# Re-ordering the interleaved attention steps of a fused attention and expert-mixture kernel: query transposes, output buffers, input sums

## Chip, cores and metric

One core of one Trainium2 chip runs the kernel. The metric is the device time of one execution in microseconds (us). TensorE is called PE, VectorE DVE, ScalarE ACT, GpSimd POOL; SyncE (SP) only issues DMAs here, and so does POOL's queue for the loads that cast from float32 to float16.

## What is computed

Attention over 4 batches of 8 heads, 768 positions, 64 wide, in 8 blocks of 96. Keys and values are first mixed across blocks by an 8 x 8 matrix per head, which comes from five rounds of exp and normalization of `sort_net`. Each block of queries then attends to its own mixed block. The output, 3072 tokens by 512, goes through four two-layer networks whose results are mixed by token weights.

```python
k_sorted = einsum('bhij,bhjcd->bhicd', P, k_b)        # P: five rounds on sort_net
v_sorted = einsum('bhij,bhjcd->bhicd', P, v_b)
scores = scale * matmul(q_b, k_sb^T)                  # per block
attn = softmax(scores)
x = matmul(attn, v_sb) -> [B * S, H * D]              # 3072 x 512
p = domain_probs / sum(domain_probs)
for e in range(4):                                    # w1: 512 x 1024, w2: 1024 x 512
    out += p[:, e] * (relu(x @ w1[e]) @ w2[e])
```

## The kernel before

**Two strands in one stream.** The networks are worked in 12 chunks: batch b (0 to 3) times c (0 to 2), 256 tokens each. While the chunks of batches 0 and 1 run, the attention of batches 1, 2 and 3 is woven between their matmuls, so that PE always has something to do. The schedule is written out by hand: instructions stand on each engine in the order of the code, each engine works in that order, and a semaphore wait of one instruction holds all behind it on the same engine.

**A chunk** (`chunk`, `chunk_first`). First the first layer: for each expert two groups of 16 matmuls (L764), each into one of two PSUM buffers of the pool psM, each evacuated by DVE with relu and token weight (L770) into `Hb`. Then the second layer as seven products over half-size blocks in the manner of Strassen (`times`, L749), into four half banks A, B, C and Q of the same two buffers, with sums of `Hb` blocks formed by DVE into `Sb` (`h_sums`, L735 to L741), and additions of the products on DVE (for batch 1: L827, L843, L844, L848, with copies on ACT at L826, L830, L835, L840). At fixed points `slot()` is called, which counts up and runs the attention steps that `PLANS` names for that count: `(c, n, step, batch, pair or half)`. With three experts (batch 0) slots 0 to 5 lie behind the groups of the first layer, with four (batch 1) slots 0 to 7; the later ones lie between the products.

**The attention steps**, per pair of heads (pr, 0 to 3):

- `st_lv`, `st_lk`, `st_n`: loads of values, keys (half a batch each) and queries (two heads each, two DMAs) into regions of the tile `arena`, on POOL's queue (L110, L121). Each region is there once, so the load of the next batch waits for the last reader of this one.
- `st_bv`, `st_bk`: the mixing matrices, built by DVE in `arena` (L335, L327).
- `st_v`: mixed values, two matmuls (L354), which ACT copies into `vo` (L360). After every second pair six DMAs on SP regroup `vo` into `vs`, the "value regroup" (L368).
- `st_q`: transposes a pair's queries from `arena` by a DMA on SP into one of three buffers qT (L375). `st_k`: mixed keys into kT, copied by ACT (L387, L396).
- `st_s`: scores, 16 matmuls (L406), and exp on ACT (L413). `st_a`: 16 matmuls with `vs` (L438), then DVE divides by the sums into `xsl` (L422, L423), one of two buffers. `st_x`: transposes `xsl` by a DMA on SP into the batch's input xT (L454); batch 3's xT lies in `room`.

Scores, outputs, mixed keys and values share a pool of two PSUM buffers, psA. SP's queue carries the regroup, all transposes, the broadcast token weights (`load_p`, L213) and the stores of the outputs (L815), in program order.

**The last six chunks** (batches 2 and 3, `last_chunk`, `seven`) use seven products for the first layer as well (L1025). For these the first-layer weights are summed once: `input_sums(e, n)`, n from 0 to 3 for each of four experts, one DVE instruction each (L961). `s1`, `s3` and `s2` go to blocks of 1024 columns of `arena` (`A_ORDER`), the fourth replaces a quarter of the weights. `PLAN_A` names the slots of batch 1's chunks in which they run, `late_sums` the places inside `last_chunk`. The input sums of expert 2 lie in columns 3072 to 6143 of `arena`, which hold the values of a batch before. `token_sums` (L980) runs in slot 12 of the last ordinary chunk, (1,2), and `last_begin` in slot 13.

```python
    def st_q(b, pr):
        qT = att.tile([P, R, P], F16, name=f"qT_{b}_{pr}", tag="qT", bufs=3)
        nc.sync.dma_start_transpose(
            qT[:], natural[(b, "q")][:, pr].rearrange("p t h d -> p (t h d)")
        )
        qTs[(b, pr)] = qT.rearrange("p t x -> p (t x)").rearrange("p (i x) -> p i x", i=NB)
```

Of the kernel before, what the change touches and what calls it, by code (L numbers as in the profile page):

```python
# [10 lines left out]
F16 = mybir.dt.float16  # L11
# [6 lines left out]
def kernel(  # L18
# [13 lines left out]
    B, H, S, D = q.shape  # L32
    GH = B * H
    NB = sort_net.shape[-1]
    BLK = S // NB
# [3 lines left out]
    P = 128  # L39
# [21 lines left out]
    att = ctx.enter_context(tc.tile_pool(name="att", bufs=2))  # L61
# [5 lines left out]
    def psa(shape, dtype, name):  # L67
        state["n"] += 1
        return psA.tile(shape, dtype, tag="ps", name=name)
# [31 lines left out]
    arena = const.tile([P, 4 * NW + NQ + 4 * 4 * P + R * 4 * VW], F16, name="arena")  # L101
# [317 lines left out]
    def normalize(ps, xsl, hh):  # L419
        av = ps[0:BLK, :, 0:HB * VW].rearrange("c a (i w) -> c a i w", w=VW)  # L420
        rz = att.tile([BLK, 2, HB, 1], F32, name=f"rz_{state['n']}", tag="rz", bufs=4)
        nc.vector.reciprocal(rz[:], av[:, :, :, D:D + 1])  # L422
        nc.vector.tensor_tensor(  # L423
            xsl[:, :, hh, :].rearrange("c (a i) d -> c a i d", a=2),
            av[:, :, :, 0:D],
            rz[:].broadcast_to([BLK, 2, HB, D]),
            ALU.mult,
        )

    def st_a(b, pr):  # L430
        xsl = att.tile([P, NB, 2, D], F16, name=f"xsl_{b}_{pr}", tag="xsl")[0:BLK]
        xsls[(b, pr)] = xsl
        vs = vss[(b, pr // 2)]
        for hh in range(2):
            ET = ETs[2 * (pr % 2) + hh]
            ps = psa([P, 2, 512], F32, f"ps_a_{b}_{pr}_{hh}")
            for i in range(NB):
                nc.tensor.matmul(  # L438
                    ps[:, i // HB, ds((i % HB) * VW, D + 1)],
                    ET[:, ds(i * BLK, P)],  # L440
                    vs[:, i, 2 * (pr % 2) + hh, 0:D + 1],
                    start=True, stop=True,
                )
            normalize(ps, xsl, hh)
# [153 lines left out]
    def st_bk(b, qd):  # L598
# [5 lines left out]
        0: [  # L604
            (0, 9, st_v, 1, 0), (0, 10, st_q, 1, 0), (0, 10, st_v, 1, 1), (0, 11, st_k, 1, 0), (0, 11, st_n, 1, 1),
            (1, 0, st_q, 1, 1), (1, 0, st_s, 1, 0), (1, 0, st_n, 1, 2), (1, 1, st_k, 1, 1), (1, 2, st_v, 1, 2),
            (1, 2, st_q, 1, 2), (1, 3, st_v, 1, 3), (1, 3, st_n, 1, 3), (1, 5, st_a, 1, 0), (1, 7, st_s, 1, 1),
            (1, 7, st_x, 1, 0), (1, 7, st_lv, 2, 0), (1, 8, st_k, 1, 2), (1, 9, st_q, 1, 3), (1, 9, st_lv, 2, 1),
            (1, 10, st_a, 1, 1), (1, 12, st_s, 1, 2), (1, 12, st_x, 1, 1), (1, 12, st_lk, 2, 0),
            (2, 0, st_k, 1, 3), (2, 0, st_n, 2, 0), (2, 0, st_n, 2, 1), (2, 0, st_n, 2, 2), (2, 0, st_n, 2, 3),  # L610
            (2, 1, st_a, 1, 2), (2, 2, st_bv, 2, 0), (2, 2, st_lk, 2, 1), (2, 3, st_s, 1, 3), (2, 3, st_x, 1, 2),
            (2, 4, st_bv, 2, 1), (2, 4, st_bk, 2, 0), (2, 6, st_v, 2, 0), (2, 7, st_a, 1, 3), (2, 8, st_v, 2, 1),
            (2, 8, st_q, 2, 0), (2, 9, st_k, 2, 0), (2, 9, st_x, 1, 3), (2, 9, st_bk, 2, 1), (2, 10, st_lv, 3, 0),
            (2, 10, st_n, 3, 0), (2, 11, st_s, 2, 0), (2, 11, st_q, 2, 1), (2, 12, st_v, 2, 2),
        ],
        1: [
            (0, 0, st_k, 2, 1), (0, 0, st_q, 2, 2), (0, 1, st_v, 2, 3), (0, 1, st_lk, 3, 0), (0, 1, st_n, 3, 1),
            (0, 2, st_a, 2, 0), (0, 2, st_q, 2, 3), (0, 2, st_lv, 3, 1), (0, 3, st_n, 3, 2), (0, 4, st_s, 2, 1),
            (0, 4, st_x, 2, 0), (0, 5, st_k, 2, 2), (0, 5, st_n, 3, 3), (0, 7, st_s, 2, 2), (0, 8, st_k, 2, 3),
            (0, 8, st_bv, 3, 0), (0, 9, st_bk, 3, 0), (0, 9, st_lk, 3, 1), (0, 9, st_q, 3, 0), (0, 10, st_a, 2, 1),  # L620
# [109 lines left out]
    def h_sums(e, which):  # L730
        blk = lambda kh, tok: Hb[:, e, ds(kh * KH, KH), ds(tok * P, P)]
        sm = [Sb[:, n, e].rearrange("p (f x) -> p f x", f=KH) for n in range(4)]
        tt = nc.vector.tensor_tensor
        if which == 1:
            tt(sm[0], blk(0, 1), blk(1, 1), ALU.add)  # L735
        elif which == 2:
            tt(sm[1], sm[0], blk(0, 0), ALU.subtract)
        elif which == 3:
            tt(sm[2], blk(0, 0), blk(0, 1), ALU.subtract)
        else:  # L740
            tt(sm[3], blk(1, 0), sm[1], ALU.subtract)  # L741

    def times(ps, lhs, rhs, es, first=True, done=True, between=None, at=None):

        for e in es:
            if e == at:
                between()
            for f in range(KH):
                nc.tensor.matmul(  # L749
                    ps, lhs(e, f), Ts[e][rhs][:, f, :],  # L750
                    start=(first and e == es[0] and f == 0), stop=(done and e == es[-1] and f == KH - 1),
                    skip_group_check=True,
                )
# [25 lines left out]
    def chunk(b, c, slot, done=()):  # L779
# [34 lines left out]
        def store(n, tile):  # L814
            nc.sync.dma_start(o[:, 2 * c + n, :], tile[:])  # L815
# [6 lines left out]
        if b:  # L822
            times(bankA, blk(0, 0), "b11", es)
            slot()
            times(bankB, blk(1, 0), "b21", es)
            nc.scalar.copy(p1[:], bankA)  # L826
            tt(oa1, bankB, p1[:], ALU.add)  # L827
            slot()
            times(bankQ, sm(0), "t1", es)
            nc.scalar.copy(p5[:], bankQ)  # L830
            slot()
            for e in es:
                h_sums(e, 3)
            times(bankA, sm(1), "t2", es, False)
            nc.scalar.copy(u2[:], bankA)  # L835
            slot()
            for e in es:
                h_sums(e, 4)
            times(bankC, blk(1, 1), "n4", es)
            nc.scalar.copy(ob1, bankC)  # L840
            slot()
            times(bankA, sm(2), "t3", es, False)
            tt(ob2, bankA, p5[:], ALU.add)  # L843
            tt(ob1, bankA, ob1, ALU.add)  # L844
            store(1, ob)
            slot()
            times(bankQ, sm(3), "b22", es, False, True, last["e0"][6] if last else None, 2 if last else None)
            tt(oa2, bankQ, u2[:], ALU.add)  # L848
            slot()
            store(0, oa)  # L850
            return
# [103 lines left out]
    def input_sums(e, n):  # L955
        a = As[e]
        dst, x, y, op = (
            ("s1", "a21", "a22", ALU.add), ("s3", "a11", "a21", ALU.subtract),
            ("s2", "s1", "a11", ALU.subtract), ("s4", "a12", "s2", ALU.subtract),
        )[n]  # L960
        nc.vector.tensor_tensor(a[dst], a[x], a[y], op)  # L961
# [3 lines left out]
    G0 = 2 * (R // 2)  # L965
# [29 lines left out]
    def prepare_last():  # L995

        last_banks(0)
        last["n"] = 1
        t = moe.tile([P, NKC, NB, BLK], F16, name="tmp7", tag="xT").rearrange("p k i x -> p (k i x)").bitcast(F32)
        room = [t[:, ds(n * 512, 512)] for n in range(3)]  # L1000
        for m in range(2):
            t = att.tile([P, NB, 4, VW], F16, name=f"tmp7_{m}", tag="vs").rearrange("p i h w -> p (i h w)")
            t = t[:, 0:2048].bitcast(F32)
            room += [t[:, 0:512], t[:, 512:1024]]
        t = att.tile([P, NB, 2, D], F16, name="tmp7_2", tag="xsl").rearrange("p i h d -> p (i h d)").bitcast(F32)
        room.append(t)
        for n, nm in enumerate(("u2", "u3", "t22", "t12")):
            last[nm] = room[2 * n:2 * n + 2]
# [67 lines left out]
    def last_begin(g):  # L1076
        last["e0"] = seven(g, 0)
        last["e0"][1]()
        last["e0"][5]()

    def last_chunk(g):
# [84 lines left out]


    PLAN_A = [
        (1, 11, 0, 0), (1, 13, 0, 1), (2, 1, 0, 2), (2, 3, 1, 0), (2, 5, 1, 1), (2, 8, 1, 2),
        (2, 9, 2, 0), (2, 10, 2, 1), (2, 11, 2, 2), (2, 11, 0, 3), (2, 12, 1, 3), (2, 13, 2, 3), (2, 13, 3, 0),  # L1170
    ]
    late_sums = {(G0, 1): [(3, 1), (3, 2)], (G0, 2): [(3, 3)]}


    mk0 = mix_half("k", 0, 0, psm, 8)
# [109 lines left out]
    for b in range(2):  # L1285
        for c in range(R // 2):
# [3 lines left out]
            def slot(b=b, c=c, at=at):  # L1290
                here = (c, at[0])
                for cc, n, f, *args in PLANS[b]:
                    if (cc, n) == here:
                        f(*args)
                if b:
                    for cc, n, e, m in PLAN_A:
                        if (cc, n) == here:
                            input_sums(e, m)
                    if here == (R // 2 - 1, 7):
                        prepare_last()  # L1300
                    if here == (R // 2 - 1, 12):
                        token_sums(G0)
                    if here == (R // 2 - 1, 13):
                        last_begin(G0)
                at[0] += 1
# [32 lines left out]
```

The softmax here doesn't subtract the row's maximum and nothing guards it: scores larger than these inputs give would overflow.

## Time and profile before

| what | value |
|---|---|
| median of 8 runs | 376.01 us (375.46 to 377.68) |
| the profiled execution | 377.04 us |
| its span, first to last instruction | 375.0 us |
| granted PE clock, mean over the span | 0.991 |
| busy PE, DVE, ACT, POOL | 359.3, 279.9, 157.7, 118.0 us |
| DMA, both directions | 38.34 MB, 69753 packets |

The profile comes from one execution, the 377.04 us one. Times in a timeline count from the start of the span. The attention of batch 1 runs from about 62 to 114 us, that of batch 2 from 109 to 157, that of batch 3 from 155 to 195; the last six chunks start at about 220. A row of a timeline gives start, length, engine, line, operation and tiles; a bracket tells how long the engine stood idle before it and what ended that. A row with xN merges N instructions. "POOL" and "SPq" rows with DMA are issues: the data lands later. The granted clock is the share of full speed that the chip allowed to PE.

### The profile page before, as it was taken

What the parts mean: (1) busy time and instruction counts of PE and PEld (TensorE: products, weight loads), DVE (VectorE), ACT (ScalarE), POOL (GpSimd) and SP (SyncE); (2) the same over time, 40 slices, a digit from 0 to 9 for tenths busy, and PEclk for the clock granted to TensorE, in tenths of its full rate; (3) what the DMA queues carried; (4) which work ended last, traced back from release to release, by engine and by line L of the source; (5) the groups of instructions that cost most, each with busy time, mean ns of one, the idle gap of its engine ahead of it and who ended that gap; (6) DMA issues with size and microseconds to landing.
All of it is one profiled execution on the core that took longest, in us unless ns stands there. A gap on an engine that the chain in (4) does not pass through costs nothing.

```text
span 375.0 us, 10552 instructions
## 1 busy us (share of the span) xinstructions
PE 359.3 (96%) x4517; PEld 317.3 (85%) x4517; DVE 279.9 (75%) x558; ACT 157.7 (42%) x282; POOL 118.0 (31%) x134
## 2 busy tenths in 40 slices
PE   8899999999995999999979999999999999999996
PEld 8786857888884788888868898999999999999995
DVE  5653898778796286867767889967968779679684
ACT  2655330543322534367400027348165283471650
POOL 8772101843200422000000005508237064181370
PEclk9999999999999899999998999999999999999999
DMA  8999999999959899925541210230110201101101
GB/s 106 206 208 231 208 209 197 192 184 213 177 91 145 143 179 108 166 73 72 102 101 21 50 65 2 34 81 2 59 58 2 93 24 58 58 3 58 58 4 54
DMA packets 69753, 38.34 MB, mean 102 GB/s; under 512 B 40390, under 2 KB 64716, under 8 KB 69708
## 3 DMA queue, kind: packets, MB, share of 16 engines
q0 software_dynamic: 34640, 17.83, 36.0%
q1 hardware_dynamic: 35068, 19.85, 26.1%
q8 instruction: 35, 0.57, 0.6%
q14 instruction: 10, 0.08, 0.1%
HBM read 42.00 MB, written 6.34 MB: 129 GB/s over the span
## 4 chain that ended last, share of the span: by engine, by line
PE 83%; DVE 6%; ACT 3%; DMA 3%; issue 2%; SPq 1%; POOL 1%; DVEq 0%; ACTq 0%; POOLq 0%
PE ps_Q L1114 20%; PE ps_h L764 19%; PE ps_p L749 11%; PE ps_X L1025 7%; PE ps_Q L1025 5%; PE ps_Z L1025 5%; PE ps_h L657 3%; PE ps_o L692 3%; PE ps_p L799 2%; PE ps_s L406 1%; DMA room<-xsl 1%; PE ps_v L354 1%; DMA qT<-arena 1%; POOL Hb L1038 1%; PE ps_a L438 1%
## 5 line engine op out<-in xcount | busy, mean ns | idle before, releaser
L1038 POOL TENSOR_TENSOR Hb<-tmp,pb 128x512 f16<-128x512 f32 x48 | 62.4, 1306 | 155.3 <-ACT tmp L1037 153.5
L764 PE MATMUL ps_h<-xT,w 128*128 128x256 f16 x672 | 80.2, 276 | 2.1 <-DVE Hb L770 2.0
L764 PEld LDWEIGHTS <-w 128*128 128x128 f16 x672 | 65.3, 99 | 11.9 <-issue 2.6
L770 DVE SCALAR_TENSOR_TENSOR Hb<-ps_h,pb 128x1024 f16<-128x1024 f32 x42 | 51.2, 1222 | 20.6 <-PE ps_h L764 20.4
L1025 PEld LDWEIGHTS <-w 128*128 128x128 f16 x768 | 46.6, 98 | 1.9 <-issue 1.2
L1114 PEld LDWEIGHTS <-Sb 128*128 128x128 f16 x384 | 37.2, 98 | 4.1
L1025 PEld LDWEIGHTS <-arena 128*128 128x128 f16 x576 | 34.7, 98 | 0.1
L1037 ACT ACTIVATE tmp<-tmp 128x512 f32<-128x512 f32 x48 | 30.5, 635 | 6.9 <-DVE tmp L1069 5.2
L121 POOL DMA_DIRECT2D arena<-in_q_dram x24 | 19.9, 840 | 39.4 <-DMA qT<-arena 30.4
L413 ACT ACTIVATE ET<-ps_s 96x768 f16<-96x768 f32 x24 | 18.0, 802 | 32.9 <-PE ps_s L406 32.6
L749 PEld LDWEIGHTS <-Sb 128*128 128x128 f16 x288 | 28.0, 100 | 4.0
L1114 PEld LDWEIGHTS <-Hb 128*128 128x128 f16 x288 | 27.4, 98 | 2.9
L1025 PE MATMUL ps_X<-kT,arena 128*128 128x128 f16 x384 | 29.3, 219 | 0.0
L396 ACT CAST kT<-ps_k 64x384 f16<-64x384 f32 x48 | 22.7, 473 | 12.6 <-PE ps_k L387 11.6
L735 DVE TENSOR_TENSOR Sb<-Hb 128x512 f16<-128x512 f16 x45 | 26.5, 609 | 0.0
L1061 DVE TENSOR_TENSOR tmp<-ps_Q,tmp 128x512 f32<-128x512 f32 x24 | 16.6, 691 | 12.9 <-ACT tmp L1060 8.5
L1114 PE MATMUL ps_Q<-w,Sb 128*128 128x256 f16 x192 | 24.7, 273 | 0.0
L1114 PE MATMUL ps_Q<-w,Hb 128*128 128x256 f16 x192 | 23.9, 273 | 0.0
L1045 ACT COPY ps_X<-ps_Z 128x512 f32<-128x512 f32 x24 | 13.7, 570 | 23.3 <-PE ps_Z L1025 22.7
L749 PEld LDWEIGHTS <-Hb 128*128 128x128 f16 x216 | 20.5, 98 | 2.8
L1114 PE MATMUL ps_Q<-T,Sb 128*128 128x256 f16 x192 | 22.9, 273 | 0.0
L1052 ACT COPY tmp<-ps_X 128x512 f32<-128x512 f32 x24 | 14.1, 586 | 12.0 <-PE ps_X L1025 12.0
(188 smaller groups left out, 610.0 us busy)
## 6 DMA issues: line engine op xcount, KB each, us to landing
w<-in_moe_w_dram POOLq DMA_DIRECT2D x7, 1024.0 KB, 26.9
pb<-p_dram SPq DMA_DIRECT2D x12, 512.0 KB, 5.8
arena<-in_k_dram POOLq DMA_DIRECT2D x8, 384.0 KB, 9.2
arena<-in_v_dram POOLq DMA_DIRECT2D x8, 384.0 KB, 8.1
vs<-arena SPq DMA_DIRECT2D x36, 66.0 KB, 4.8
arena<-in_q_dram POOLq DMA_DIRECT2D x24, 96.0 KB, 6.8
out_dram<-ob SPq DMA_DIRECT2D x9, 256.0 KB, 2.0
out_dram<-oa SPq DMA_DIRECT2D x8, 256.0 KB, 2.4
```

The costliest lines, as they stand in the source:

```text
L121: nc.gpsimd.dma_start(t[:, h // 2, :, h % 2, :], q[b, h].rearrange("(t p) d -> p t d", p=P))
L396: nc.scalar.copy(kT[ds(D * hh, D), r], pk[ds(D * r, D), hh].rearrange("p a (i c) -> p a i c", c=CP),)
L413: nc.scalar.activation(ETs[2 * (pr % 2) + hh][:, 0:S].rearrange("c (a x) -> c a x", a=2), pss[hh][0:BLK, :, 0:HS], AF.Exp, bias=0.0, scale ...
L735: tt(sm[0], blk(0, 1), blk(1, 1), ALU.add)
L749: nc.tensor.matmul(ps, lhs(e, f), Ts[e][rhs][:, f, :], start=(first and e == es[0] and f == 0), stop=(done and e == es[-1] and f == KH - 1 ...
L764: nc.tensor.matmul(ps[:, f, :], w1sb[e][:, kc, ds((4 * g + f) * P, P)], xT[:, kc, ds(2 * c * P, 2 * P)], start=(kc == 0), stop=(kc == NKC ...
L770: nc.vector.scalar_tensor_tensor(out=Hb[:, e, ds(4 * g, 4), :], in0=ps[:], scalar=0.0, op0=ALU.max, in1=pb[:, ds(e, 1), :].broadcast_to([P ...
L1025: nc.tensor.matmul(dst[:, ds(f * P, P)], a[lhs][:, k, ds(f * P, P)], t[rhs][:, k, :], start=(first and f == 0 and k == 0), stop=(f == KH - ...
L1037: nc.scalar.activation(src, src, AF.Relu, bias=0.0, scale=1.0)
L1038: nc.gpsimd.tensor_tensor(Hb[:, e, ds(i * KH, KH), ds(j * P, P)], src.rearrange("p (f x) -> p f x", f=KH), pb[:, ds(e, 1), ds(j * P, P)].b ...
L1061: tt(t22, Q, u3, ALU.add)
L1114: nc.tensor.matmul(ps, lhs(e, f), Ts[e][rhs][:, f, :], start=(first and e == 0 and f == 0), stop=(e == E - 1 and f == KH - 1), skip_group_ ...
```

## The change

Four things, all of them places and order; each engine has the same instructions as before.

1. The outputs of pairs 2 and 3 of batch 3 go to columns 4096 to 6143 of `arena`, which held values of batch 3, instead of to the two `xsl` buffers.
2. The query transposes of pairs 0 and 1 of batch 2 move from slots (2,8) and (2,11) to (2,4) and (2,5) of batch 0's last chunk, ahead of both value steps and their regroup; pair 2's moves from the first slot of batch 1 to (2,12). The query loads of batch 2 (`st_n`) are spread over slots (2,0) and (2,1).
3. Outputs (`st_a`) and scores (`st_s`) of batch 1 move by a slot here and there; in batch 1's chunks the slot behind product B now comes ahead of ACT's copy and DVE's first addition (L826, L827).
4. Input sums move to earlier slots: (1,2), (2,0) to (2,2), (0,3), (1,3) by one slot, (3,0) and (2,3) change places, (3,1) and (3,2) from inside the first of the last chunks to slots 13 and 14 ahead of it, and (3,3) from its expert 2 to its expert 3.

```diff
     def st_a(b, pr):
-        xsl = att.tile([P, NB, 2, D], F16, name=f"xsl_{b}_{pr}", tag="xsl")[0:BLK]
+        if b == B - 1 and pr >= H // 2 - 2:
+            xsl = arena[:, ds((pr + 2) * NB * 2 * D, NB * 2 * D)].rearrange("p (i h d) -> p i h d", i=NB, h=2)[0:BLK]
+        else:
+            xsl = att.tile([P, NB, 2, D], F16, name=f"xsl_{b}_{pr}", tag="xsl")[0:BLK]
...
-            (1, 2, st_q, 1, 2), (1, 3, st_v, 1, 3), (1, 3, st_n, 1, 3), (1, 5, st_a, 1, 0), (1, 7, st_s, 1, 1),
-            (1, 7, st_x, 1, 0), (1, 7, st_lv, 2, 0), (1, 8, st_k, 1, 2), (1, 9, st_q, 1, 3), (1, 9, st_lv, 2, 1),
-            (1, 10, st_a, 1, 1), (1, 12, st_s, 1, 2), (1, 12, st_x, 1, 1), (1, 12, st_lk, 2, 0),
-            (2, 0, st_k, 1, 3), (2, 0, st_n, 2, 0), (2, 0, st_n, 2, 1), (2, 0, st_n, 2, 2), (2, 0, st_n, 2, 3),
-            (2, 1, st_a, 1, 2), (2, 2, st_bv, 2, 0), (2, 2, st_lk, 2, 1), (2, 3, st_s, 1, 3), (2, 3, st_x, 1, 2),
-            (2, 4, st_bv, 2, 1), (2, 4, st_bk, 2, 0), (2, 6, st_v, 2, 0), (2, 7, st_a, 1, 3), (2, 8, st_v, 2, 1),
-            (2, 8, st_q, 2, 0), (2, 9, st_k, 2, 0), (2, 9, st_x, 1, 3), (2, 9, st_bk, 2, 1), (2, 10, st_lv, 3, 0),
-            (2, 10, st_n, 3, 0), (2, 11, st_s, 2, 0), (2, 11, st_q, 2, 1), (2, 12, st_v, 2, 2),
+            (1, 2, st_q, 1, 2), (1, 3, st_v, 1, 3), (1, 3, st_n, 1, 3), (1, 6, st_a, 1, 0), (1, 7, st_lv, 2, 0),
+            (1, 8, st_s, 1, 1), (1, 8, st_x, 1, 0), (1, 9, st_k, 1, 2), (1, 9, st_q, 1, 3), (1, 9, st_lv, 2, 1),
+            (1, 11, st_a, 1, 1), (1, 12, st_lk, 2, 0),
+            (2, 0, st_s, 1, 2), (2, 0, st_x, 1, 1), (2, 0, st_n, 2, 0), (2, 0, st_n, 2, 1), (2, 1, st_k, 1, 3),
+            (2, 1, st_n, 2, 2), (2, 1, st_n, 2, 3), (2, 2, st_bv, 2, 0), (2, 2, st_lk, 2, 1), (2, 2, st_a, 1, 2),
+            (2, 4, st_s, 1, 3), (2, 4, st_x, 1, 2), (2, 4, st_bv, 2, 1), (2, 4, st_bk, 2, 0), (2, 4, st_q, 2, 0),
+            (2, 5, st_q, 2, 1), (2, 6, st_v, 2, 0), (2, 7, st_a, 1, 3), (2, 8, st_v, 2, 1), (2, 9, st_k, 2, 0),
+            (2, 9, st_x, 1, 3), (2, 9, st_bk, 2, 1), (2, 9, st_lv, 3, 0), (2, 9, st_n, 3, 0), (2, 11, st_s, 2, 0),
+            (2, 12, st_v, 2, 2), (2, 12, st_q, 2, 2),
         ],
         1: [
-            (0, 0, st_k, 2, 1), (0, 0, st_q, 2, 2), (0, 1, st_v, 2, 3), (0, 1, st_lk, 3, 0), (0, 1, st_n, 3, 1),
+            (0, 0, st_k, 2, 1), (0, 1, st_v, 2, 3), (0, 1, st_lk, 3, 0), (0, 1, st_n, 3, 1),
...
             times(bankB, blk(1, 0), "b21", es)
+            slot()
             nc.scalar.copy(p1[:], bankA)
             tt(oa1, bankB, p1[:], ALU.add)
-            slot()
             times(bankQ, sm(0), "t1", es)
...
     PLAN_A = [
-        (1, 11, 0, 0), (1, 13, 0, 1), (2, 1, 0, 2), (2, 3, 1, 0), (2, 5, 1, 1), (2, 8, 1, 2),
-        (2, 9, 2, 0), (2, 10, 2, 1), (2, 11, 2, 2), (2, 11, 0, 3), (2, 12, 1, 3), (2, 13, 2, 3), (2, 13, 3, 0),
+        (1, 11, 0, 0), (1, 13, 0, 1), (2, 1, 0, 2), (2, 3, 1, 0), (2, 5, 1, 1), (2, 7, 1, 2),
+        (2, 8, 2, 0), (2, 9, 2, 1), (2, 10, 2, 2), (2, 10, 0, 3), (2, 11, 1, 3), (2, 11, 3, 0), (2, 12, 2, 3),
+        (2, 13, 3, 1), (2, 14, 3, 2),
     ]
-    late_sums = {(G0, 1): [(3, 1), (3, 2)], (G0, 2): [(3, 3)]}
+    late_sums = {(G0, 3): [(3, 3)]}
```

## The prediction

> **What bounds the kernel now.** I read the page first, then the waits of the PE, then the timelines around each wait, then the stretches (busy time and granted clock).
>
> ```profile
> span 375.0 us, 10552 instructions
> ...
> PE 359.3 (96%) x4517; PEld 317.3 (85%) x4517; DVE 279.9 (75%) x558; ACT 157.7 (42%) x282; POOL 118.0 (31%) x134
> ...
> PE 83%; DVE 6%; ACT 3%; DMA 3%; issue 2%; SPq 1%; POOL 1%; DVEq 0%; ACTq 0%; POOLq 0%
> ```
>
> TensorE is busy for 96% of the span and is 83% of the chain that ended last. The change neither adds nor removes an instruction on any engine (the changed program's order has the same rows, moved), so only idle time of the PE, and its clock, can change. The waits of the PE between 80 and 240 us:
>
> ```profile
> PE ps_s L406 <- DMA qT<-arena: 4.9, 1, 4.9
> PE ps_h L764 <- DVE Hb L770: 2.0, 1, 2.0
> PE ps_Q L1025 <- DVE tmp L1061: 0.8, 1, 0.8
> PE ps_s L406 <- DVE xsl L423: 0.6, 2, 0.4
> ```
>
> The second number counts waits. That is 8.3 us, and two of these waits also cost clock. The stretches, cut where the clock changes (columns: stretch, length, busy time of PE, PEld, DVE, ACT, POOL, clock, DMA share, GB/s):
>
> ```profile
> 119.50:122.92 3.42, 0.47 (x17) 0.42 (x18) 0.00 (x0) 0.00 (x0) 0.07 (x1) 1.00 1.21 188
> 122.92:126.33 3.41, 3.41 (x19) 2.28 (x17) 0.42 (x1) 1.50 (x2) 1.57 (x2) 0.50 1.20 163
> ...
> 194.60:198.01 3.41, 1.37 (x14) 1.08 (x12) 3.38 (x6) 0.00 (x0) 0.00 (x0) 1.00 0.43 77
> 198.01:201.42 3.41, 3.41 (x19) 2.35 (x17) 2.02 (x3) 0.00 (x0) 0.00 (x0) 0.50 0.00 1
> ```
>
> After each of the two long waits the clock is 0.50 for 3.41 us: 1.7 us of work lost each time. So the waits and their clock together hold 8.3 + 3.4 = 11.7 us, the most the change could win.
>
> **Part 1: outputs of pairs 2 and 3 of batch 3 go to the arena.** The wait at 194.76 starts on VectorE:
>
> ```profile
> 191.65 0.20 DVE L422 RECIPROCAL rz<-ps_a 96x8 f32<-96x8 f32 x1
> 194.10 0.69 DVE L423 TENSOR_TENSOR xsl<-ps_a,rz 96x512 f16<-96x512 f32 x1 [2.26 <-DMA room<-xsl]
> 194.70 0.19 DVE L422 RECIPROCAL rz<-ps_a 96x8 f32<-96x8 f32 x1
> ...
> 195.54 2.34 DVE L770 SCALAR_TENSOR_TENSOR Hb<-ps_h,pb 128x1024 f16<-128x1024 f32 x2
> ```
>
> L423 of pair 3 waits 2.26 us until the transpose of pair 1 (issued at 189.55, 4.45 us to landing) gives its buffer back. The two L770 evacuations stand behind it, and the PE needs the first one's bank at 194.76; it resumes at 196.80. With space of its own, pair 3's four instructions follow L848 at 191.65 and take what pair 2's took, 189.04 to 190.71, so 1.67 us, to 193.32. The first L770 (2.34 / 2 = 1.17) ends at 194.49, before 194.76. The second starts with its matmuls' end and is done by 196.0; the PE needs it at 196.5. Next late is DVE itself, by a margin of 0.27 us: if it slips more, the PE waits for the excess. The wait (2.04) goes, and the half clock with it: 96 matmuls took 12.36 us there, against 10.5 at the usual 1.75 per 16, so 1.86. **-3.9 us**, if all of it goes; from the other side 0, if another DVE delay of over 2 us takes its place, for which I see no row. The new space is read by the transposes alone until input sums (2,1) and (2,2) write it some 15 us later, and was last read by the value matmuls near 176.9, so no wait enters.
>
> By the Trainium skill, "TensorE: Matmul & The Clock Gate", Part 1, the gate closes after an idle window of about 3.4 us, free-running, and gaps under that are safe. By it this 2.04 us gap would cost no clock and part 1 would be worth 2.0. The row with 1.37 us busy of 3.41, followed by 0.50, says otherwise; I go by the row. (The window before 119.50 had 1.44 busy, and was not followed by half clock.)
>
> **Part 2: query transposes of pairs 0 and 1 of batch 2, from slots (2,8) and (2,11) to (2,4) and (2,5).** SP now:
>
> ```profile
> 114.56 3.78 SPq L368 DMA_DIRECT2D vs<-arena  x6
> 118.45 1.25 SPq L375 DMA_TRANSPOSE qT<-arena  x1
> 119.79 1.23 SPq L454 DMA_TRANSPOSE xT<-xsl  x1
> 121.19 1.22 SPq L375 DMA_TRANSPOSE qT<-arena  x1
> ```
>
> The scores of pair 0 could start at 117.37 but wait to 122.45 for the transpose that stands behind the six regroup copies. Moved, both transposes are issued near 106 and 107, right behind pair 2's output transpose (today SP issues nothing from 104.0 to 110.08), and the query loads, the last issued at 99.83 and landing in 4 to 5 us, are in. This wait goes. **What is late next is xT of pair 3 of batch 1.** Chunk (1,0) needs it after its first three matmuls, and it stands right behind the same regroup. Today it hides: the PE reaches that point at 126.08. Without the wait the PE reaches it after 16 scores (0.45), 12 matmuls (1.31) and 2 value matmuls (0.33) from 117.1: at 119.2.
>
> When does xT land? It takes the place of the first query transpose. The regroup starts 0.3 earlier (DVE, 9.87 us busy of 10 before 110, passes on only 0.3 of what parts 3 and 4 free), at 114.26. Today the transpose in that place lands 3.9 us after 118.45, so 7.8 us after the first copy: 122.0. But the move also releases something: POOL's two query loads of batch 3, today issued at 122.85 after 8.11 us of waiting for this very transpose, now follow the value load at 114.00 and share the DMA engines, whose share is already 1.2 there. The nearest row with such a load is the next regroup at 131.44, with a value load and four query DMAs beside it: six copies at 4.9 to 7.7 us, and the transpose behind them (136.26 + 7.05) landing 11.9 us after the first copy. So xT lands between 122.0 and 126.1; with two of the four query DMAs, 7.8 + 2.05 us after 114.26: **124.1**.
>
> "DMA: Bandwidth & Descriptors", section Queues, rings and completion order, says each engine round-robins between queues, packet by packet: SP's copies would slow by no more than the bytes beside them, which is what the 131.44 row shows too. It speaks against this move being free.
>
> The first group of chunk (1,0) then ends at 124.1 + 13 matmuls (1.42) + half clock again (1.7, the gap of 4.5 us being longer than both seen) = 127.2; today it ends at 127.95. **-0.75 us** where 6.6 (4.9 + 1.7) seemed to be on offer. Ends: 122.0 and no half clock, -4.5; 126.1, +1.3.
>
> The third transpose (pair 2) is issued near 120 instead of 126.64, for scores that come 15 us later: nothing. Other queues: pb's copy (110.08) stays where VectorE lets it; POOL's later loads wait for matmuls as now. The regroup also holds `vo`, into which ACT writes the next values: ACT would wait to about 123.5, while the PE is waiting anyway.
>
> **Part 3: outputs and scores of batch 1 re-spaced by half a slot or one slot; slot() of L829 ahead of the copy L826 and the addition L827.** The two waits of L406 for xsl (0.40 at 87.46 and 0.21 at 181.38) go, since a product of 1.31 to 1.75 us now stands between. The first only moves the PE nearer to part 2's wait and is in its 0.3. The second counts: **-0.2**. In chunk (1,0) L827 follows a build of 0.6 us; its bank was freed by ACT, nobody waits. In chunk 2 of batch 1 two sums (1.2 us) precede L827, where DVE idles 1.18 today.
>
> **Part 4: input sums earlier.** At 227.60 to 229.56 VectorE runs two L961 (1.35 and 0.68) ahead of L1061, for which the PE waits 0.80. They move to before the last chunks: one into 0.70 us of idle before L848, one after it, which makes the next L1031 0.45 late; L1061 behind that idles 1.02 today, so it is covered. L1061 then starts when ACT's copy (227.74 + 0.59) ends, at 228.35, and is done by 229.0; the PE wants it at 229.41. **-0.8**. The last sum (3,3), 0.85 us, goes to where DVE has slack until p3 of expert 3 at 236.50.
>
> **Sum.** 3.9 + 0.75 + 0.2 + 0.8 = 5.65. The profiled execution took 377.04 us (span 375.0 and 2.0 around it), so 371.4. The median of the runs is 376.01, 1.03 lower. Part of what I take away, the clock after a gap as short as 2.04, is what one run may have and another not; I therefore let the 1.03 come off the gain and predict **371.4** for the median too. If it is the same overhead in both, 370.4.
>
> **Rivals.**
> - *The released query loads don't hurt* (0.2): xT lands at 122.0. For it: the first copies at 114.56 already suffered a value load. Then the group ends at 122.0 + 1.42 + 1.7 = 125.1, 2.1 better: 369.3; without half clock 367.6.
> - *Part 1 is half cured* (0.14): DVE's margin of 0.27 is lost, or the median runs had no half clock there (1.86): 373.3.
> - *No change* (0.04): xT at 126.1 (+2.0) and part 1's clock not won (+1.86): 375.3.
> - *Slower* (0.05): the value and query loads keep SP's queue off the engines. The place is xT at the start of chunk (1,0). Faster by 4.9 elsewhere, the change loses once the group there ends later than 127.95 + 4.9, so xT later than 129.7, 15.4 us after the first copy. The longest such row has 11.9, single query loads had up to 13.6 at 82.88. At 131.5: 378.8.
> - My forecast has 0.57, with 370 to 373 as its own range.
>
> Two measurements of this kernel can be told apart from 0.3% (1.1 us). Faster by more: 0.57 + 0.2 + 0.14 = 0.91; within: 0.04; slower: 0.05. The range runs from the first rival without half clock, nearly, to the half-cured case with xT late: 368 to 374.3.
>
> **What would show it.** In the changed profile: no wait of L423 for a transpose and no wait of L764 for L770 near 194, no half clock near 198; the wait of L406 for qT gone, and in its place a wait of L764 for the DMA xT<-xsl of 2 to 6 us at the start of chunk (1,0), followed by half clock; POOL's query loads right behind the value load at 114; no wait of L1025 for L1061 at 230. Wrong if that new wait is absent or longer than 7 us, or if a wait for VectorE stands where part 1 took one away.

## The result

Measured in turn, the changed kernel takes **371.74 us** (370.30 to 373.59, 11 runs) and the kernel before 376.23 us (374.96 to 377.99, 32 runs): ratio 0.9882, 95% interval 0.9865 to 0.9900. It is faster, by 4.5 us; 371.4 was forecast. The profiled execution took 371.1 us.

### The profile page after: what moved, and what is told of

The parts are those of the page before. It is cut to its first block, busy times and chain, and to the rows that moved or that the text cites. A ratio compares the mean times of both kernels' runs of the same rounds, so it can differ in the third digit from the quotient of the medians.

```text
span 369.0 us, 10554 instructions
## 1 busy us (share of the span) xinstructions
PE 356.8 (97%) x4517; PEld 316.0 (86%) x4517; DVE 279.7 (76%) x558; ACT 157.4 (43%) x282; POOL 117.9 (32%) x134
## 3 DMA queue, kind: packets, MB, share of 16 engines
HBM read 42.00 MB, written 6.34 MB: 131 GB/s over the span
## 4 chain that ended last, share of the span: by engine, by line
PE 83%; DVE 6%; POOL 4%; issue 2%; DMA 2%; ACT 1%; POOLq 0%; ACTq 0%; DVEq 0%
PE ps_Q L1118 19%; PE ps_h L768 19%; PE ps_p L753 12%; PE ps_X L1029 7%; PE ps_Z L1029 5%; PE ps_Q L1029 5%; PE ps_h L661 3%; PE ps_o L696 3%; POOL Hb L1042 2%; PE ps_p L803 2%; DMA xT<-xsl 2%; PE ps_s L406 1%; PE ps_k L387 1%; PE ps_a L441 1%; DVE Hb L774 1%
## 5 line engine op out<-in xcount | busy, mean ns | idle before, releaser
L768 PE MATMUL ps_h<-xT,w 128*128 128x256 f16 x672 | 80.6, 277 | 4.6 <-DMA xT<-xsl 4.5
L768 PEld LDWEIGHTS <-w 128*128 128x128 f16 x672 | 65.5, 99 | 14.2 <-issue 4.7
L774 DVE SCALAR_TENSOR_TENSOR Hb<-ps_h,pb 128x1024 f16<-128x1024 f32 x42 | 51.3, 1222 | 25.1 <-PE ps_h L768 24.9
L1065 DVE TENSOR_TENSOR tmp<-ps_Q,tmp 128x512 f32<-128x512 f32 x24 | 16.6, 692 | 13.8 <-ACT tmp L1064 8.7
```

Of the source, the lines that this page charges most:

```text
L768: nc.tensor.matmul(ps[:, f, :], w1sb[e][:, kc, ds((4 * g + f) * P, P)], xT[:, kc, ds(2 * c * P, 2 * P)], start=(kc == 0), stop=(kc == NKC ...
L774: nc.vector.scalar_tensor_tensor(out=Hb[:, e, ds(4 * g, 4), :], in0=ps[:], scalar=0.0, op0=ALU.max, in1=pb[:, ds(e, 1), :].broadcast_to([P ...
L1065: tt(t22, Q, u3, ALU.add)
```

## The profile after

The page: span, busy times and the chain by engine, in the form shown of before.

```profile
span 369.0 us, 10554 instructions
...
PE 356.8 (97%) x4517; PEld 316.0 (86%) x4517; DVE 279.7 (76%) x558; ACT 157.4 (43%) x282; POOL 117.9 (32%) x134
...
PE 83%; DVE 6%; POOL 4%; issue 2%; DMA 2%; ACT 1%; POOLq 0%; ACTq 0%; DVEq 0%
```

The work is the same; only idle time and clock of the PE changed. The waits of the PE between 80 and 240 us:

```profile
PE ps_h L768 <- DMA xT<-xsl: 4.5, 1, 4.5
PE ps_Q L1029 <- DVE tmp L1065: 0.2, 1, 0.2
PE ps_v L354 <- DVE xsl L423: 0.2, 1, 0.2
```

Line numbers are four higher than before: L768 is the former L764, L774 the former L770, L1065 the former L1061. The four waits of before (8.3 us) are gone, but for 0.2 us behind the addition (L1065, the former L1061), which now fall an expert later, at 230.5. In their place stands the one that the prediction names as late next, and it is nearly as long as the wait for qT was. The stretches around it, and the two around 198 (columns as in the prediction):

```profile
117.74:121.15 3.41, 0.96 (x8) 0.61 (x7) 0.42 (x1) 0.49 (x1) 0.00 (x0) 1.00 1.73 177
121.15:124.56 3.41, 1.38 (x7) 0.98 (x7) 0.00 (x0) 0.80 (x1) 0.00 (x0) 0.50 1.07 246
124.56:127.98 3.42, 3.42 (x21) 2.56 (x20) 1.22 (x1) 1.14 (x3) 0.91 (x2) 0.50 0.00 0
194.60:198.01 3.41, 3.41 (x34) 3.06 (x32) 3.22 (x5) 0.00 (x0) 0.00 (x0) 1.00 0.03 5
198.01:201.42 3.41, 3.41 (x33) 2.99 (x32) 3.41 (x6) 0.00 (x0) 0.00 (x0) 1.00 0.00 0
```

Around 198 the PE is busy without a break at full clock. But the clock is 0.50 from 121.15 to 127.98: two windows, where before had one there. The timelines of PE, SP and ACT at that place, one fence each:

```profile
118.21 0.49 PE L768 MATMUL ps_h<-xT,w 128*128 128x256 f16 x3
123.18 2.93 PE L768 MATMUL ps_h<-xT,w 128*128 128x256 f16 x13 [4.49 <-DMA xT<-xsl]
```

```profile
113.22 4.02 SPq L368 DMA_DIRECT2D vs<-arena  x6
117.34 1.34 SPq L457 DMA_TRANSPOSE xT<-xsl  x1
118.78 0.53 SPq L819 DMA_DIRECT2D out_dram<-room  x1
```

```profile
122.77 0.80 ACT L360 CAST arena<-ps_v 128x768 f16<-128x768 f32 x1 [4.54 <-DMA vs<-arena]
```

xT's transpose still stands behind the six regroup copies; it lands at 123.14, and the PE goes on at 123.18 with 13 matmuls in 2.93 us, where the forecast has 1.42 for them at full clock. ACT waits for the regroup alongside.

To see where each microsecond went, I laid the start of every matmul of one trace beside the start of the same matmul of the other, and read how far the changed kernel is ahead. Each trace is one execution; "in the traces" means this comparison of two of them, here and below.

| at, in the changed kernel | ahead by, us | step |
|---|---|---|
| 21 | 1.29 | start-up, untouched by the change |
| 113 | 1.34 | |
| scores of batch 2, pair 0 (116.1) | 6.34 | wait for qT gone |
| third matmul of chunk (1,0) (118.4) | 8.00 | half clock of before not there yet |
| fourth matmul (123.18) | 3.35 | new wait for xT |
| 129 | 1.04 | two windows at half clock |
| 181 | 1.45 | part 3 |
| 200 | 5.30 | part 1 |
| 224 | 6.28 | part 4 |
| 237, and the end | 5.97 | part 4, the part given back |

The 1.29 us of the start-up are scatter between two executions. The change holds 4.7 of the 6.0 us between the spans, and the medians differ by 4.5.

## Experiments

**Theories.** Mine: of the two long waits one (part 1) is really cured, the other (part 2) is handed to the next transfer behind the same regroup, together with its half clock; the released query loads push that transfer late. Rivals: both parts help, or the gain comes from parts 3 and 4.

### Part 1 alone

The kernel before with the first hunk of the diff and nothing else:

```diff
+        if b == B - 1 and pr >= H // 2 - 2:
+            xsl = arena[:, ds((pr + 2) * NB * 2 * D, NB * 2 * D)].rearrange("p (i h d) -> p i h d", i=NB, h=2)[0:BLK]
```

> The kernel before with part 1 alone: outputs of pairs 2 and 3 of batch 3 in the arena. My theory (the wait of 2.0 us near 194 and the half clock after it, 1.9 us, both go): 3.9 us less than before, 372.3 us; no wait of L770's matmuls, no half clock near 198; the waits near 117 (4.9) and 230 (0.8) stay. Rival, that a gap this short costs no clock in most runs: 2.0 us less, 374.2. Rival, that another DVE delay takes its place: less than 1 us.

Measured: 372.99 us against 376.11, ratio 0.9922 (0.9895 to 0.9948), so 2 to 4 us: the times fit both my 3.9 and the rival's 2.0, and don't decide between them. They do rule out that another delay takes the place of this one. The PE's timeline at the place (its profile, of the slowest of the 12 runs, 376.94, which had a half clock of its own from 75.93 to 79.34):

```profile
195.18 14.18 PE L767 MATMUL ps_h<-xT,w 128*128 128x256 f16 x128
```

All 128 matmuls of the layer in one stretch; the kernel before has a gap of 2.04 us and a half clock in it. In the traces the place gains 3.85 us, and the waits for qT and for L1064 are as before.

### Part 2 alone

```diff
-(2, 8, st_q, 2, 0), ... (2, 11, st_q, 2, 1), ... (0, 0, st_q, 2, 2)
+(2, 4, st_q, 2, 0), (2, 5, st_q, 2, 1), ... (2, 12, st_q, 2, 2)
```

> The kernel before with part 2 alone: query transposes of pairs 0 to 2 of batch 2 in their new slots, query loads where they were. My theory (the wait for the query transpose is replaced by one for xT of pair 3 of batch 1, which lands near 124, with half clock as before or longer): between 0.8 us less and 0.8 us more than before, 375.4 to 377. Rival, that the removed wait is won: 4.9 to 6.6 us less, 369.6 to 371.3. Rival, that part 2 only helps with the re-spaced slots: slower by over 1 us.

Measured: 375.27 us, ratio 0.9994 (0.9969 to 1.0019). The waits of the PE in its profile:

```profile
PE ps_h L764 <- DMA xT<-xsl: 6.1, 1, 6.1
PE ps_h L764 <- DVE Hb L770: 2.3, 1, 2.3
PE ps_Q L1025 <- DVE tmp L1061: 0.8, 1, 0.8
```

The wait for qT (4.9) has become one for xT (6.1): moving the transposes alone wins nothing. The rival by which part 2 carries the gain falls. That parts 3 and 4 carry it does not fit with part 1 alone, which leaves them what is missing to 4.5; in the traces they hold 1.1. Part 3 was not run by itself.

### The query loads held back

The changed kernel with the query loads of batch 3's pair 0, which the move lets out at 113.4, put behind the next key load, after the regroup:

```diff
-(2, 9, st_n, 3, 0),
+(0, 1, st_lk, 3, 0), (0, 1, st_n, 3, 0), (0, 1, st_n, 3, 1),
```

> The changed kernel, with the two query loads of batch 3's first pair moved behind the next key load, so that they no longer follow the value load near 113 and do not share the DMA engines with the regroup and with xT. Theory that these loads delay xT: it lands some 2 us earlier, 4 to 4.5 us after its issue at most, the PE waits 2 to 2.7 instead of 4.5, and the time falls by 2 to 3 us from 371.7, to 369 or 370. Rival, that only xT's place behind the regroup counts: landing 5.8 us after issue as now, wait 4.5, 371.7. Rival, that the held loads make the next burst of DMAs late: wait shorter here, but a new wait 10 to 25 us later, and no gain.

Measured: 370.52 us, ratio 0.985 (0.9821 to 0.9879). The interval overlaps that of the changed kernel (0.9865 to 0.9900), so the times don't settle it; the traces do. The last regroup copy lands 7.3 us after the first is issued instead of 9.5. But xT lands 9.3 us after it instead of 9.9, and the PE waits 3.9 instead of 4.5 us. So my theory on the cause of the late xT is mostly wrong, as far as one trace each can tell: the loads delay the regroup by 2 us, but xT by 0.6.

### The store behind it moved away

In both, SP issues an output store right behind xT's transpose. In these two the query transpose of pair 2 goes ahead of that store, once with the loads held and once without:

```diff
-(2, 9, st_x, 1, 3), ... (2, 12, st_q, 2, 2),
+(2, 9, st_x, 1, 3), (2, 9, st_q, 2, 2),
```

> The changed kernel with the query loads of batch 3 held (as in the run of that name) and, besides, the query transpose of pair 2 moved from slot (2,12) to right behind the output transpose of pair 3 of batch 1, so that SP issues transpose, transpose, store instead of transpose, store, transpose. With the loads held alone, xT landed 5.4 us after its issue and 2.0 after the regroup's last copy. Theory: the output store issued 0.1 us behind xT's transpose shares the DMA engines with it; with another transpose there instead, xT lands 3.9 us after its issue as the query transpose did in the kernel before, and the wait of L768 for xT falls from 3.9 to about 2.4. Rival: the store does not matter, the landing stays at 5.4 and the wait at 3.9. One run; its time is read for nothing under 1 us.

> The changed kernel with only the query transpose of pair 2 moved ahead of the output store, query loads where the change puts them. Theory: both the store and the query loads delay xT, so it lands between the changed kernel's 9.9 us and 7.8 us after the first regroup copy, about 9.0, and the wait falls from 4.5 to 3.6. Rival, the store alone makes the difference to the kernel before: 7.8 us after the first copy, a wait of 2.4. Second rival, no effect: 9.9 and 4.5.

One run each, 371.06 and 372.13 us. With the loads held, xT landed 5.3 us after its issue (5.4 before the store was moved) and the wait was 3.7; without, 6.7 after it, and the wait was 5.2. So these two traces show no gain from moving the store either. What the DMA view of the first of the two shows from 118 to 124 us (40 slices of 0.15 us: busy tenths, then GB/s):

```profile
DMA  9999999999999995799990001010069999998999
GB/s 331 335 243 176 176 159 173 178 216 202 188 206 186 171 114 26 162 359 278 266 55 0 0 0 9 7 10 9 10 131 128 229 380 437 437 437 328 382 423 410
...
q8 instruction: 1, 0.02, 1.1%
```

From 121.0 to 122.4 the 16 DMA engines move almost nothing, though xT's transpose is pending; it lands at 122.85, when they move again. In the trace 21 packets of 256 bytes begin there within 0.05 us and last until 122.46. 0.44 us ahead of them, at 120.56, the instruction queue (q8) fetched 16 KB. The changed kernel has a similar picture: fetch at 120.12, packets held from 120.7 to 122.4, xT at 123.14. In the kernel before, the fetch came at 125.47, behind the transposes. With the loads held and the store in its place it is there too: fetch at 120.99, almost nothing moves from 121.5 to 122.7, xT at 123.35. So at this place a pause of 1.2 to 1.7 us stands beside the fetch. That the fetch is its cause was not tried, and one trace has a shorter pause without one: in the run of part 2 alone 15 such packets are held for 1.1 us from 105.58 on, with no fetch between 99.31 and 108.64.

### The transpose first

If what stands ahead of xT makes it late, xT should go ahead. Pair 3 is divided and in `xsl` by 112.7 in the changed kernel, so its transpose can be issued before the regroup:

```diff
-(2, 7, st_a, 1, 3), (2, 8, st_v, 2, 1), ... (2, 9, st_x, 1, 3),
+(2, 7, st_a, 1, 3), (2, 8, st_x, 1, 3), (2, 8, st_v, 2, 1),
```

> The changed kernel with the output transpose of pair 3 of batch 1 issued ahead of the second value step and its regroup instead of behind them. Theory that the new wait comes from xT's place behind the regroup: the wait of 4.5 us at the start of chunk (1,0) and its half clock (2.4) go. What is late next is vo: ACT's copy of the next values waits for the regroup, some 0.5 us later than the 122.8 of now, so the value matmuls of pair 3 find no free buffer at 122.0 and wait some 2 us. Net 2.5 to 4.5 us less than the changed kernel's 371.7: 367 to 369. Rival, that the regroup behind it is delayed by so much that the new wait is as long as the old: 371 to 372. Rival, that xT is held by the loads anyway: wait of 2 us or more for xT stays.

Measured: **365.81 us**, ratio 0.9711 (0.9694 to 0.9729), better than I had put it. The PE there, from its timeline:

```profile
119.11 2.03 PE L768 MATMUL ps_h<-xT,w 128*128 128x256 f16 x16
120.98 0.50 PE L387 MATMUL ps_k<-arena 128*128 128x128 f16 x6
121.31 1.91 PE L768 MATMUL ps_h<-xT,w 128*128 128x256 f16 x16
124.69 0.48 PE L354 MATMUL ps_v<-arena 128*128 128x384 f16 x2 [1.47 <-ACT arena L360]
```

The first group follows without a wait, at full clock; xT landed at 119.52. What is late next is the regroup itself, for which ACT waits and behind ACT the PE, 1.47 us. With the query loads held as well, both edits together:

> The kernel of the run with the output transpose first, and the two query loads held back behind the next key load. If the loads slow the regroup by the 1.35 us seen when they were held alone (last copy landing at 121.3 against 122.7), the wait for vo and its buffers shrinks to under 1 us and the time falls a further 1 to 1.5 us: 366 to 367.5. Rival, that the burst which then carries the held loads (127 to 140 us) becomes the bound: a new wait there and no further gain.

> The fast version once more, on the same chip as the two kernels that undo one part of it: 365.6, from 365.3 to 366.0, as in its first runs.

Measured: **365.62 us**, ratio 0.9705 (0.9692 to 0.9718), and again 364.94, ratio 0.970 (0.968 to 0.972). The waits from 100 to 240 us (first of the two):

```profile
PE ps_h L768 <- DMA xT<-xsl: 0.5, 1, 0.5
PE ps_Q L1029 <- DVE tmp L1065: 0.2, 1, 0.2
PE ps_v L354 <- DVE xsl L423: 0.2, 1, 0.2
```

The wait of 4.5 is 0.5 and no half clock is left: in the traces 6.3 us less than the changed kernel from 113 to 128, which is the 3.9 of the wait and the 2.3 of the clock. This is the best version, some 6 us under the changed kernel. The loads held add too little to the first edit to be told apart by the times.

### The clock by itself

The changed kernel with 64 matmuls of the identity in the gap, into a bank that the next group overwrites; they compute nothing that is used:

```diff
+                if (b, c, e, g) == (1, 0, 0, 0):
+                    for _ in range(64):
+                        nc.tensor.matmul(ps[:, 0, 0:P], ident, ident, start=True, stop=True)
```

> The changed kernel with 64 extra matmuls of 128 x 128 (ident by ident, into the bank that the first group then overwrites, so they leave the output as it is) ahead of the first group of chunk (1,0). They take 3.6 us of the gap in which the PE waits for xT and move no DMA. Theory that half clock follows idleness: the wait shrinks to about 1.3 us, xT lands as now, the half clock (2.4 us lost in the changed profile) goes, and the time falls by 1.7 to 2.4 us to 369.3 to 370. Rival, that the clock falls for another reason or that the gap alone counts: 371.7, with half clock as now.

Measured: 370.72 us, ratio 0.9858 (0.9828 to 0.9887). The PE's timeline:

```profile
119.30 3.74 PE L768 MATMUL ps_h<-ident 128*128 128x128 f16 x64
122.88 0.49 PE L771 MATMUL ps_h<-xT,w 128*128 128x256 f16 x3
124.29 1.58 PE L771 MATMUL ps_h<-xT,w 128*128 128x256 f16 x13 [0.92 <-DMA xT<-xsl]
```

xT is no earlier, but the 13 matmuls behind it take 1.58 us instead of 2.93, and over the place the kernel gains 2.3 us on the changed one in the traces. So 2.3 us of what the new wait costs is clock, and the clock follows the PE's idleness. (0.55 of it is lost again by 170 us, 0.36 of that in a wait for a copy by ACT.) The times alone (intervals overlap) would not show it, but the mean clocks of the runs agree: 0.999 or 1.0 in four of these six and 0.995 in two, against 0.986 to 0.995 in all twelve of the changed kernel.

### The best version without part 1, and without part 4

The best version with one part undone each: outputs of batch 3 in `xsl` again, and `PLAN_A` and `late_sums` of before.

```diff
-        if b == B - 1 and pr >= H // 2 - 2:
-            xsl = arena[:, ds((pr + 2) * NB * 2 * D, NB * 2 * D)].rearrange("p (i h d) -> p i h d", i=NB, h=2)[0:BLK]
```

```diff
-    late_sums = {(G0, 3): [(3, 3)]}
+    late_sums = {(G0, 1): [(3, 1), (3, 2)], (G0, 2): [(3, 3)]}
```

> The fast version (output transpose ahead of the regroup, query loads held; 365.6 us in its first runs) with part 1 undone: all outputs of batch 3 in the two xsl buffers again. Theory: the wait of about 2.0 us of L774 for the buffer of a transpose comes back near 189, and the PE works at half clock for one window of 3.41 us behind it, so 365.6 + 3.85 = 369.5 (mean clock 0.995). Rival: a gap of 2.0 to 2.3 us does not always close the clock, since the run of the query transposes alone had a gap of 2.29 us there and full clock behind it; then only the wait comes back: 367.6 (clock 0.999 or 1.0). Both may appear among the runs, and then the clock of each run tells which it was, with 1.7 us between them.

> The fast version with the input sums (part 4) back in the slots of the kernel before. Theory: part 4 is worth the 0.67 us that the traces show between 220 and 237 us (wait for the addition behind the two sums 0.8 gone, 0.2 to 0.3 back one expert later): 366.3. Rival, part 4 gains nothing, since sums that no longer run there only push the same VectorE work to the place where the PE waits next: 365.6.

Measured, on the chip of the second run of the best (364.94): without part 1 367.34 us, ratio 0.9779 (0.9752 to 0.9807); without part 4 365.60, ratio 0.9718 (0.9697 to 0.9739). The PE without part 1, and a stretch laid around its gap:

```profile
189.01 10.69 PE L765 MATMUL ps_h<-xT,w 128*128 128x256 f16 x96 [2.19 <-DVE Hb L771]
```

```profile
186.40:189.80 3.40, 1.21 (x12) 0.93 (x11) 3.37 (x5) 0.00 (x0) 0.00 (x0) 1.00 0.45 87
189.80:193.20 3.40, 3.40 (x34) 3.05 (x32) 2.94 (x5) 0.00 (x0) 0.00 (x0) 1.00 0.10 18
```

The wait is back (2.19), but the 96 matmuls behind it take 10.69 us, at full clock; before they took 12.36. The stretches above are not the windows of the clock; cut by the grid described in the last section, the gap falls into two of them, and the emptier, from 187.18 to 190.59, still has 1.58 us of PE work. The rival is right for four of the five runs: part 1 is worth 2.4 us here. The fifth, with a mean clock of 0.995, took 369.17. Part 4 shows 0.66 in the medians and a wait of 0.8 for L1065 back in the profile, as the theory has it, but the intervals overlap; the time itself (365.60) is the one that the rival had named.

### The last sum one expert earlier

```diff
-    late_sums = {(G0, 3): [(3, 3)]}
+    late_sums = {(G0, 2): [(3, 3)]}
```

> The changed kernel with input sum (3,3) back at expert 2 of the first of the last chunks. Theory that the sum at its new place (1.24 us, ahead of the addition for which the PE waits) costs the 0.3 us seen at 230.5: the wait of 0.23 there goes. At its old place it stands where DVE idles 0.7, so a wait of up to 0.5 may come at 227 instead. Rival, that the additions are late for another reason: wait of 0.2 as now. The time of one run tells nothing at this size.

One run, 373.97 us; 2.3 us of it, a wait of 1.7 for a qT among them, come before 75 us, which this edit doesn't touch. VectorE and PE at the place:

```profile
228.35 1.31 DVE L965 TENSOR_TENSOR w<-w,arena 128x1024 f16<-128x1024 f16 x1
229.59 0.68 DVE L1065 TENSOR_TENSOR tmp<-ps_Q,tmp 128x512 f32<-128x512 f32 x1
```

```profile
230.32 0.61 PE L1029 MATMUL ps_Q<-xT,w 128*128 128x128 f16 x8 [0.19 <-DVE tmp L1065]
```

The sum stands an expert earlier, and so does the wait (0.19; 0.23 in the changed kernel). So at both places that were tried the sum costs these 0.2 us, and the theory that the later place is to blame falls.

## Why the prediction was right

| term | forecast, us | in the traces, us |
|---|---|---|
| part 1 | -3.9 | -3.85 |
| part 2 | -0.75 | +0.30 |
| part 3 | -0.2 | -0.41 |
| part 4 | -0.8 | -0.67 |
| sum | -5.65 | -4.63 |

**Part 1** came as worked out, in the trace; the median of part 1 alone gives 3.1. VectorE after:

```profile
190.19 0.19 DVE L422 RECIPROCAL rz<-ps_a 96x8 f32<-96x8 f32 x1
190.42 0.69 DVE L423 TENSOR_TENSOR arena<-ps_a,rz 96x512 f16<-96x512 f32 x1
191.03 0.19 DVE L422 RECIPROCAL rz<-ps_a 96x8 f32<-96x8 f32 x1
191.26 0.69 DVE L423 TENSOR_TENSOR arena<-ps_a,rz 96x512 f16<-96x512 f32 x1
191.86 1.21 DVE L774 SCALAR_TENSOR_TENSOR Hb<-ps_h,pb 128x1024 f16<-128x1024 f32 x1
```

From 190.19 to 191.86 are 1.67 us, the forecast to the hundredth, and the evacuation follows without a wait. But its 1.86 us of clock are not a fixed price: in the profiled runs of part 2 alone and of the best version without part 1 the gap was longer (2.29 and 2.19) and the clock stayed full.

**Part 2**: the wait for qT went, xT was late next, the query loads followed the value load at once, and the PE waited 4.5 us at the start of chunk (1,0). xT landed 9.92 us after the first copy; 9.85 was forecast. Three things in it were off:

- *Mis-sized:* "half clock again (1.7, ...)". Two windows fell, not one, and cost 2.3. That is 0.6 of the 1.05 us between the forecast and the traces. The reason given, a gap "longer than both seen", misreads the lines: one of the two was 4.9 us, and it cost one window.
- *Mis-sized:* "The regroup starts 0.3 earlier". It was issued at 113.22 instead of 114.56, and 1.29 of these 1.34 us are the start-up, so 0.05. That is 0.25 more.
- *Right in size, wrong in cause:* "with two of the four query DMAs, 7.8 + 2.05 us". The loads held back gave 0.6 of it. The rest goes with the pause of the DMA engines shown above, which stands beside an instruction fetch; what causes it stays open. The sum came right by luck: the loads do hold the regroup up by 2 us, but with them gone the pause holds xT up instead.

**Parts 3 and 4** came within about 0.2. The 0.3 that part 4 gives back at the last sum was put at nothing ("to where DVE has slack"); there is no slack there (a wait of 0.23), nor an expert earlier (0.19 in the run with that sum moved).

**The median.** I let the 1.03 us between the profiled run of before and the median come off the gain, for the clock that one run has and another not. The number came right, and by luck: the traces hold 1.02 us less than the sum of the terms (4.63 for 5.65), because part 2 lost where it was to win, and the 1.03 taken off for another reason, a clock that part 1 might not win, fills just this gap. With the same overhead in both, as the prediction's other reading has it, 370.4 would have been 1.3 too low. The profiled run of before was indeed slow, but in its start-up: of the 14 traces its start-up is the longest and that of the changed kernel the shortest (1.29 us apart), with the others between. How far the clock has a share in the medians stays open.

## What to carry to other kernels

When a wait behind a queue's batch of copies goes, look at the next transfer in that queue: here it inherited the wait, and nothing was won until that one moved ahead too (0.9994 alone, and 6 us more with xT's transpose first). Where a buffer's release waits for a DMA, giving the writer dead space elsewhere can take out the whole wait, as the 2.04 us did here. Price an idle gap of the PE by where it may fall among the clock's windows, as two prices with chances, not as one.

## What the hardware showed unexpectedly

**The windows.** In these traces the clock changes only on a grid of 3.41 us, whose place differs from run to run. Cut on that grid, the busy time of the PE in a window tells the clock of the next. In the run of part 2 alone:

```profile
117.64:121.06 3.42, 1.49 (x13) 1.08 (x12) 0.78 (x2) 1.01 (x2) 0.00 (x0) 1.00 1.83 168
121.06:124.47 3.41, 0.00 (x0) 0.00 (x0) 0.00 (x0) 0.09 (x1) 0.00 (x0) 1.00 1.33 149
124.47:127.88 3.41, 2.68 (x13) 1.87 (x13) 0.00 (x0) 0.71 (x1) 0.00 (x0) 0.50 0.42 128
...
192.74:196.15 3.41, 1.98 (x19) 1.63 (x17) 1.82 (x4) 0.00 (x0) 0.00 (x0) 1.00 0.51 118
196.15:199.56 3.41, 2.55 (x24) 2.28 (x24) 3.14 (x4) 0.00 (x0) 0.00 (x0) 1.00 0.32 60
```

A window with 0.00 busy is followed by half clock; one with 1.49, and the two between which the 2.29 us gap is split, are not. Over all the kept traces, from 10 us on, full-clock windows with at most 1.37 us busy (0.00, 0.30, 0.47, 0.51, 0.82, 0.96, 1.19, 1.27, 1.37) were followed by 0.50, those with 1.44 or more (1.44, 1.49, 1.58, 1.98, 2.55 among them) were not. A window that was itself at half clock needed more: with 1.38, 1.45, 1.77 and 1.86 another at 0.50 followed (in the changed kernel, and in the runs with the last sum moved, the loads held, and loads held and store later); with 2.68 none did. So a gap of just over 2 us costs clock if it falls whole into one window and not if it is split between two, and the gaps of 4.5 to 4.9 cost one window or two. The Trainium skill ("TensorE: Matmul & The Clock Gate", Part 1) says that the window is free-running, which these traces agree with, and that the gate closes after an idle window; here a window that was 40% busy (1.37 of 3.41) was enough.

**The landing of a transpose** came no sooner after its issue when nothing stood ahead of it on SP: put first, it still landed 6.0 to 7.0 us after it in all five traces (3.9 for the query transpose behind the copies in before), each time 0.2 to 0.4 us after the value load that POOL issued beside it. What won was the earlier issue (113.57 instead of 117.34 in the first of them). Whether it waits for that load was not tried.
